# A chunk's input load in three column pieces of 48 rows instead of three row pieces of 16

## The chip, the cores and the metric

The kernel runs on one core of one Trainium2 chip. The core has five engines that run their own instruction lists: TensorE (PE, matrix products; its weight loads are listed as PEld), VectorE (DVE), ScalarE (ACT), GpSimd (POOL) and SyncE (SP), which here issues nearly all DMA transfers. Engines wait for each other and for transfers on semaphores. The metric is the device time of one execution in microseconds (us).

## What is computed

A recurrent attention over 768 steps for 4 batches of 8 heads, and after it a gated layer on its output. The reference, cut to what matters (`w_in`, `w_spatial`, `b_spatial` and `w_out` are the layer's weights):

```python
# r, k, v, w, a, b: (4, 8, 768, 40); state: (B, H, 40, 40), zero at first
for t in range(S):
    y[:, :, t] = einsum('bhd,bhde->bhe', rt, state)
    Sa = einsum('bhde,bhe->bhd', state, at)
    state = state * wt[:, :, None, :] - einsum('bhd,bhe->bhde', Sa, bt)
    state = state + einsum('bhd,bhe->bhde', vt, kt)
x = y.transpose(0, 2, 1, 3).reshape(B, S, H * D)
h = maximum(x @ w_in, 0)
u, v = h[..., :512], h[..., 512:]
v_n = (v - mean(v)) / sqrt(var(v) + 1e-6)          # over the last axis
v_s = einsum('ts,bsd->btd', w_spatial, v_n) + b_spatial[None, :, None]
out = (u * v_s) @ w_out
```

## The kernel before

The recurrence is done in chunks of 64 steps. There are two groups of two batches and 12 chunks each, so 24 chunks, `s` = 0 to 23; a chunk holds 8 units of a batch and a pair of heads, and the two heads of a pair (`par` 0 and 1) lie on the two halves of the partitions, from 0 and from 64 on, in 40 rows each.

Each chunk goes through three kinds of work. The **preparation** (`scan1`, `scan2`, `scr_store`, `at_mul`, `sl_mul`, `lprime`, `lblock`) takes the chunk's input tile `ein` (128 x 2064 floats): columns 0 to 527 (`W`) are the decays, the next 512 the vectors a, the last 1024 the vectors b and k. `scan1` (L288) and `scan2` (L297) run over the decays on VectorE, `at_mul` (L314) multiplies the a columns with the result, `sl_mul` (L320) the last columns, and `lprime` (L335) makes 32 x 32 blocks of their products on TensorE, which ScalarE copies out (`lblock`, L345). Every four chunks VectorE inverts these blocks in some 60 small steps (`invert`, L351 to L373). The **b_ work** makes the chunk's matrices, and the **c_ work** carries the state on from chunk to chunk: `c_bp` (L532), `c_ff` (L550), `c_xx` (L568), `c_mp` (L596, L607) and `c_y` (L618, L631), with copies on ScalarE and masks on GpSimd (`strict`, L405). Decoding of the weights and the first product of the gated layer (L676 to L739) are put in between, and a second phase (L100 to L202), on TensorE above all, follows.

There are four `ein` buffers for chunks 0 to 3. From chunk 4 on two are used in turn, `ein0` for even and `ein1` for odd chunks. Chunks 4 and 5 are loaded whole by `prep_load` (L270). From chunk 6 on `prep_piece` (L275) loads a chunk in six DMAs of SP: `k % 2` is the half of the partitions, `k // 2` the third of it. The pieces of chunk `q + 2` go into the buffer that chunk `q` leaves, so they are planned behind `sl_mul` of chunk `q`.

The order on each engine is set by the planned times in `at(t, ...)`: all calls are sorted by `t` and written out in that order. One unit of `t` is one chunk of the c_ work. The preparation of chunks 4 to 11 is planned two chunks per unit, later ones one per unit. SP works off its DMAs in order and stands still at one whose semaphores aren't there yet, for what its target is still read for and for an earlier DMA that used the same one of eight semaphores.

Of the kernel before, what the change touches and what calls it, by code (L numbers as in the profile page):

```python
# [19 lines left out]
C = 64  # L20
# [4 lines left out]
NU = NB * NP  # L25
GS = 4
WSEG = C + 2
WF = NU * WSEG
EW = WF + 3 * NU * C
# [187 lines left out]
def phase1(ctx, tc, early, late, vtok, win, xs, vns, uts, dscr):  # L217
    nc = tc.nc
# [32 lines left out]
    ein = [p.tile([P, EW], F32, name=f"ein{i}") for i, p in enumerate((pin, pin, extra, extra))]  # L251
# [18 lines left out]
            queues[par].dma_start(out=t[o:o + rows, cols], in_=early[par, s, 0:rows, cols])  # L270

    def prep_piece(s, k):
        par, r = k % 2, k // 2 * 16
        o = par * 64 + r
        nc.sync.dma_start(out=ein[s % 2][o:o + 16], in_=early[par, s, r:r + 16])  # L275

    def scan1(s, i=None):
        t = ein[s % 2 if i is None else i]
# [529 lines left out]
    for q in range(GS, NS):  # L808
        t = PREP.get(q, q - 8 + 0.01)
        at(OV.get((scan1, q), t + 0.20), scan1, q)  # L810
        at(OV.get((scan2, q), t + 0.28), scan2, q)
        at(OV.get((scr_store, q), t + 0.285), scr_store, q)
        at(OV.get((at_mul, q), t + 0.29), at_mul, q, AT_ENG)
        at(OV.get((sl_mul, q), t + 0.30), sl_mul, q, SL_ENG)
        if q + 2 < NS:
            gap = GAP.get(q, 0.07 if q < 12 else 0.14)
            for k in range(6):
                at(max(t + 0.40, OV.get((sl_mul, q), 0) + 0.01) + gap * k, prep_piece, q + 2, k)
        at(t + LPQ.get(q, LPO), lprime, q)
        at(t + LPQ.get(q, LPO) + 0.05, lblock, q)  # L820
# [168 lines left out]
```

## Time and profile before

| | |
|---|---|
| Time, median of 3 runs | 661.7 us (660.37, 661.7 and 666.66) |
| Profiled execution | 664.58 us, of which the span of the trace is 662.9 us |
| Busy share of the span | PE 87%, PEld 79%, DVE 67%, ACT 59%, POOL 34% |
| Mean granted TensorE clock | 0.941 of full speed |
| DMA | 87.68 MB in 106,587 packets, mean 132 GB/s |
| Chunk pieces (L275) | 108 DMAs of 129.0 KB |

How to read it: the busy shares are averages over the whole execution, whose stages have different limits, so a stage is looked at by itself. A matmul's end is modelled, so a busy TensorE isn't one at its peak. [...] An idle time in brackets stands just before the row's instruction, with what ended it.

### The profile page before, as it was taken

Reading aid. Unit: us, or ns where it says so; the run is one execution under the profiler, and the core shown is the slowest. Engines: PE = TensorE matmul, PEld = TensorE weight load, DVE = VectorE, ACT = ScalarE, POOL = GpSimd, SP = SyncE. Lnnn points to the kernel's source line nnn. Section 1 sums busy time; section 2 is a strip of 40 time slices with the busy share of each in tenths; the row PEclk is TensorE's granted clock in tenths of the full one; section 3 lists DMA queues with packets and bytes.
Section 4 is the critical chain, followed back from the end, with each engine's and each line's share of the span. In section 5 each row is a group of like instructions: output and inputs, shape, how many; then the busy total and the mean of one; then the engine's idle time right before and its main releaser. Section 6 shows DMA issues by size and latency. Waiting matters only on the chain.

```text
span 662.9 us, 25888 instructions
## 1 busy us (share of the span) xinstructions
PE 577.4 (87%) x10960; PEld 523.0 (79%) x10960; DVE 445.2 (67%) x951; ACT 394.3 (59%) x884; POOL 225.2 (34%) x312
## 2 busy tenths in 40 slices
PE   1628876478788888999999999999999999999998
PEld 1527766367677777888888888888888999999997
DVE  8898559978999999689787666443375844322221
ACT  2226654358676777788878888888774643232112
POOL 3113213104323334352341342323344935352121
PEclk9977787869798889999999999999999999999999
DMA  8754866458574756656666356365386558150001
GB/s 201 125 101 65 137 140 128 91 123 137 125 160 120 147 111 141 133 141 147 158 179 179 82 144 172 83 168 164 100 238 196 170 165 250 49 169 31 31 30 60
DMA packets 106587, 87.68 MB, mean 132 GB/s; under 512 B 35752, under 2 KB 92328, under 8 KB 104552
## 3 DMA queue, kind: packets, MB, share of 16 engines
q1 hardware_dynamic: 105928, 84.31, 52.4%
q10 hardware_dynamic: 544, 1.72, 1.1%
q8 instruction: 86, 1.41, 1.0%
q14 instruction: 29, 0.24, 0.1%
HBM read 59.20 MB, written 20.50 MB: 120 GB/s over the span
## 4 chain that ended last, share of the span: by engine, by line
PE 67%; DVE 13%; issue 7%; ACT 5%; DMA 5%; SPq 2%; POOL 1%; DVEq 0%; ACTq 0%; POOLq 0%
PE po L199 6%; PE pv L736 6%; PE pv L689 6%; PE pg L179 5%; PE pg L181 5%; PE pg L180 5%; PE bp L532 5%; PE ch L550 4%; PE ch L568 4%; PE bk L422 3%; PE bk L438 3%; DVE itmp L362 3%; PE bk L398 3%; DMA ein<-in_early 3%; DVE A L366 2%
## 5 line engine op out<-in xcount | busy, mean ns | idle before, releaser
L405 POOL TENSOR_SCALAR_AFFINE_SELECT Rt<-Rt 64x512 f32<-64x512 f32 (+1 forms) x144 | 83.8, 583 | 149.1 <-ACT Rt L578 113.6
L405 POOL TENSOR_SCALAR_AFFINE_SELECT At<-At 64x512 f32<-64x512 f32 x48 | 40.3, 840 | 149.9 <-ACT At L414 137.5
L362 DVE TENSOR_TENSOR itmp<-A 128x30 f32<-128x30 f32 (+9 forms) x180 | 68.7, 382 | 3.5
L542 ACT ACTIVATE Rt<-bp 64x416 f32<-64x416 f32 x96 | 49.1, 512 | 35.0 <-PE bp L532 33.2
L179 PE MATMUL pg<-wsh,vh 128*128 128x384 f32 x192 | 64.5, 336 | 1.1 <-ACT vh L51 1.1
L183 DVE TENSOR_TENSOR g<-pg,bb 128x384 f32<-128x384 f32 x32 | 17.8, 556 | 70.6 <-PE pg L181 67.9
L180 PE MATMUL pg<-wsl,vh 128*128 128x384 f32 x192 | 64.4, 335 | 0.0
L366 DVE TENSOR_TENSOR A<-A,itmp 128x30 f32<-128x30 f32 (+9 forms) x180 | 59.1, 328 | 6.1
L181 PE MATMUL pg<-wsh,vl 128*128 128x384 f32 x192 | 63.1, 336 | 0.0
L532 PE MATMUL bp<-lin,Mc 40*64 40x104 f32 x768 | 47.7, 280 | 16.7 <-DVE y L631 14.2
L532 PEld LDWEIGHTS bp<-lin,Mc 40*64 40x64 f32 x768 | 40.9, 151 | 20.2 <-DVE y L631 17.1
L55 POOL TENSOR_TENSOR gl<-g,gh 128x384 fp32r<-128x384 f32 x32 | 33.7, 1056 | 57.5 <-ACT gh L51 57.5
L578 ACT ACTIVATE Rt<-ch 64x416 f32<-64x416 f32 x96 | 49.2, 512 | 5.1 <-PE ch L568 2.7
L550 PE MATMUL ch<-Rt,At 128*64 128x104 f32 x768 | 46.9, 281 | 3.4 <-issue 2.6
L51 ACT ACTIVATE gh<-g 128x384 fp32r<-128x384 f32 x32 | 16.7, 522 | 54.5 <-DVE g L184 54.5
L550 PEld LDWEIGHTS ch<-Rt,At 128*64 128x64 f32 x768 | 41.3, 155 | 7.5 <-issue 4.2
L335 PE MATMUL bk<-at,sl 64*32 64x32 f32 x1536 | 22.4, 208 | 28.1 <-DVE sl L320 15.9
L335 PEld LDWEIGHTS bk<-at,sl 64*32 64x32 f32 x1536 | 18.7, 119 | 31.4 <-issue 13.2
L568 PE MATMUL ch<-ffs,xf 64*64 64x104 f32 x768 | 43.2, 267 | 0.0
L55 POOL TENSOR_TENSOR vl<-raw,vh 128x512 fp32r<-128x512 f32 x24 | 31.7, 1333 | 29.4 <-ACT vh L51 27.3
L607 DVE TENSOR_TENSOR Mc<-ch,scn 104x160 f32<-104x160 f32 x44 | 18.6, 439 | 32.8 <-PE ch L596 26.2
L568 PEld LDWEIGHTS ch<-ffs,xf 64*64 64x64 f32 x768 | 38.3, 144 | 1.1
(128 smaller groups left out, 1508.7 us busy)
## 6 DMA issues: line engine op xcount, KB each, us to landing
ein<-in_early SPq DMA_DIRECT2D x108, 129.0 KB
lin<-in_late SPq DMA_DIRECT2D x48, 160.0 KB
At<-at SPq DMA_DIRECT2D x48, 128.0 KB
uts<-ur SPq DMA_DIRECT2D x48, 128.0 KB
vns<-vr SPq DMA_DIRECT2D x24, 256.0 KB
raw<-vns SPq DMA_DIRECT2D x24, 256.0 KB
ut<-uts SPq DMA_DIRECT2D x24, 256.0 KB
Rt<-in_vtok SPq DMA_DIRECT2D x48, 80.0 KB
```

Of the source, the lines that this page charges most:

```text
L55: eng.tensor_tensor(out=lo, in0=x, in1=hi.bitcast(F32), op=ALU.subtract)
L179: nc.tensor.matmul(pg, lhsT=vh[:, dc], rhs=w_h, start=(i == 0), stop=False)
L180: nc.tensor.matmul(pg, lhsT=vh[:, dc], rhs=w_l, start=False, stop=False)
L181: nc.tensor.matmul(pg, lhsT=vl[:, dc], rhs=w_h, start=False, stop=(i == NT - 1))
L362: nc.vector.tensor_tensor(out=tp, in0=A[:, k + 1:, k:k + 1].broadcast_to([P, m, k]), in1=A[:, k:k + 1, 0:k].broadcast_to([P, m, k]), op=AL ...
L366: nc.vector.tensor_tensor(out=A[:, k + 1:, 0:k], in0=A[:, k + 1:, 0:k], in1=tp, op=ALU.add)
L405: nc.gpsimd.affine_select(out=t, in_=t, pattern=[[0, k], [1, C]], base=0, channel_multiplier=-1, compare_op=ALU.is_gt, fill=0.0,)
L532: nc.tensor.matmul(bp[PR[par], q, :], lhsT=Mc[RR[par], n, :], rhs=li[RR[par], n, C:], start=(q == 0), stop=False, skip_group_check=True,)
L542: nc.scalar.activation(Rt[par][PR[par], gp, :], st["bp", g][PR[par]], AF.Copy)
L550: nc.tensor.matmul(ff[PR[1 - par], q, :], lhsT=At[par][:, n, :], rhs=Rt[par][:, n, :], start=True, stop=True,)
L568: nc.tensor.matmul(xx[ev, q, :], lhsT=xf[ev, n, :], rhs=ffs[ev, q, :], start=True, stop=True,)
L578: done = nc.scalar.activation(Rt[par][PR[par], gp], xx[PR[1 - par]], AF.Copy, scale=-1.0)
```

## The change

The six pieces of a chunk's load are cut in another way. Before, a piece was 16 of the 48 rows of one half, in full width (16 x 2064 floats, 132 KB). After, it is all 48 rows of one half in one of three ranges of columns: 528 for the scans, 512 for the first product, 1024 for the last one (101, 98 and 197 KB). The two halves still alternate, and each piece has the planned time that it had.

```diff
     def prep_piece(s, k):
-        par, r = k % 2, k // 2 * 16
-        o = par * 64 + r
-        nc.sync.dma_start(out=ein[s % 2][o:o + 16], in_=early[par, s, r:r + 16])
+        par, cols = k % 2, (slice(0, WF), slice(WF, WF + NU * C), slice(WF + NU * C, EW))[k // 2]
+        o = par * 64
+        nc.sync.dma_start(out=ein[s % 2][o:o + 48, cols], in_=early[par, s, 0:48, cols])
```

On SP, at the place where chunk 6 (`ein_120`) is loaded, the rows of before (-) and of the change (+); in brackets are the semaphores a DMA waits for, where DMAHW ones belong to earlier DMAs and DVE is VectorE:

```order
-L275 DMA ein_120<-in_early 16x2064 [waits DMAHW2_49,DVE_49]
-L275 DMA ein_120<-in_early 16x2064 [waits DMAHW3_49]
-L275 DMA ein_120<-in_early 16x2064 [waits DMAHW4_49]
-L275 DMA ein_120<-in_early 16x2064 [waits DMAHW5_49]
-L275 DMA ein_120<-in_early 16x2064 [waits DMAHW6_49]
-L275 DMA ein_120<-in_early 16x2064 [waits DMAHW7_49]
+L275 DMA ein_120<-in_early 48x528 [waits DMAHW2_49,DVE_49]
+L275 DMA ein_120<-in_early 48x528 [waits DMAHW3_49]
+L275 DMA ein_120<-in_early 48x512 [waits DMAHW4_49,DVE_49]
+L275 DMA ein_120<-in_early 48x512 [waits DMAHW5_49]
+L275 DMA ein_120<-in_early 48x1024 [waits DMAHW6_49,DVE_49]
+L275 DMA ein_120<-in_early 48x1024 [waits DMAHW7_49]
```

The six stay where they were; the wait for VectorE stood on the first of them alone and now stands on the first of each pair.

On VectorE, at the preparation of the same chunk:

```order
-L288 SCALAR_TENSOR_TENSOR S<-ein_120,ends 128x528 [waits DMAHW5_49,DMAHW4_49,DMAHW6_49,DMAHW3_49,DMAHW7_49,DMAHW2_49,Activation_49]
+L288 SCALAR_TENSOR_TENSOR S<-ein_120,ends 128x528 [waits DMAHW3_49,DMAHW2_49,Activation_49]
 L292 RECIPROCAL ends<-S 128x8 [waits DVE_49]
 L297 SCALAR_TENSOR_TENSOR Et<-ein_120,ends 128x528 [waits DVE_49]
-L314 TENSOR_TENSOR at<-ein_120,Et 128x512 [waits DVE_49]
-L320 TENSOR_TENSOR sl<-ein_120,S 128x1024
+L314 TENSOR_TENSOR at<-ein_120,Et 128x512 [waits DMAHW5_49,DMAHW4_49,DVE_49]
+L320 TENSOR_TENSOR sl<-ein_120,S 128x1024 [waits DMAHW7_49,DMAHW6_49]
```

The first scan waited for six transfers and now waits for two; the two products each wait for two of their own. The order of VectorE, TensorE, ScalarE and GpSimd is the same in both kernels.

## Rows read from the trace of the kernel before

**Rows 1.** Windows: busy us (x instructions) of each engine, granted clock, DMA share, GB/s.
```profile
core 0: us, PE busy (x) PEld busy (x) DVE busy (x) ACT busy (x) POOL busy (x), PEclk, DMA share, GB/s
65.00:95.00 30.00, 23.06 (x661) 20.44 (x651) 15.85 (x20) 17.42 (x40) 6.71 (x11) 0.86 0.81 138
95.00:130.00 35.00, 23.41 (x624) 20.57 (x622) 32.86 (x77) 16.52 (x39) 9.46 (x18) 0.82 0.58 119
...
207.00:240.00 33.00, 27.53 (x696) 24.56 (x698) 31.65 (x59) 22.46 (x52) 8.00 (x16) 0.79 0.55 123
...
280.00:340.00 60.00, 60.00 (x1500) 52.89 (x1496) 49.73 (x123) 50.60 (x119) 21.52 (x34) 1.00 0.62 151
```

**Rows 2.** VectorE's timeline, 55 to 118 us: start, us, instruction [idle before, releaser].
```profile
55.25 1.26 DVE L297 TENSOR_TENSOR_SCAN Et<-ein,ends 128x528 f32<-128x528 f32 x1
...
64.67 0.42 DVE L631 TENSOR_TENSOR y<-bp,Et 104x256 f32<-104x256 f32 x1 [0.67 <-PE bp L618]
67.01 1.26 DVE L288 TENSOR_TENSOR_SCAN S<-ein,ends 128x528 f32<-128x528 f32 x1 [1.92 <-DMA ein<-in_early]
...
70.44 1.69 DVE L320 TENSOR_TENSOR sl<-ein,S 128x1024 f32<-128x1024 f32 x1
73.44 1.26 DVE L288 TENSOR_TENSOR_SCAN S<-ein,ends 128x528 f32<-128x528 f32 x1 [1.30 <-DMA ein<-in_early]
...
82.52 0.44 DVE L607 TENSOR_TENSOR Mc<-ch,scn 104x160 f32<-104x160 f32 x1 [4.43 <-ACT zt L483]
...
95.16 1.95 DVE L351 STREAM_TRANSPOSE A<-Lc 128x1024 f32<-128x1024 f32 x1 [5.23 <-ACT Lc L345]
...
117.73 1.25 DVE L288 TENSOR_TENSOR_SCAN S<-ein,ends 128x528 f32<-128x528 f32 x1
```

**Rows 3.** VectorE's waits, 60 to 345 us: total us, times, longest us.
```profile
DVE S L288 <- DMA ein<-in_early: 3.2, 2, 1.9
```

**Rows 4.** TensorE's waits, 60 to 345 us, those marked "issue".
```profile
PE bk L335 <- issue: 8.7, 6, 2.1
...
PE ch L550 <- issue: 2.6, 1, 2.6
PE bp L532 <- issue: 2.0, 1, 2.0
...
PE bk L398 <- issue: 1.6, 1, 1.6
```

**Rows 5.** Queue q8 (packets, MB, share of 16 engines), 64:69 and 83:87 us.
```profile
q8 instruction: 1, 0.02, 2.1%
...
q8 instruction: 1, 0.02, 1.9%
```

**Rows 6.** The same queue, 50 to 56 us.
```profile
q8 instruction: 1, 0.02, 1.0%
```

**Rows 7.** Windows by what the DMA engines carry: last two columns DMA share, GB/s.
```profile
0.00:16.00 16.00, 2.50 (x128) 2.06 (x128) 13.24 (x21) 4.34 (x10) 6.59 (x15) 1.00 0.88 201
29.00:43.00 14.00, 9.02 (x168) 8.47 (x164) 12.86 (x34) 6.95 (x15) 2.67 (x4) 0.98 0.95 163
63.00:73.00 10.00, 7.76 (x225) 6.96 (x223) 6.45 (x8) 5.54 (x12) 4.38 (x5) 0.84 1.02 138
```

**Rows 8.** SP's timeline: start, us in all, DMA issues.
```profile
24.73 1.41 SPq L270 DMA_DIRECT2D ein<-in_early  x2
...
58.40 2.64 SPq L275 DMA_DIRECT2D ein<-in_early  x6
...
63.84 4.41 SPq L275 DMA_DIRECT2D ein<-in_early  x6
...
69.56 1.17 SPq L391 DMA_DIRECT2D At<-at  x2
...
103.23 4.78 SPq L275 DMA_DIRECT2D ein<-in_early  x4
```

**Rows 9.** TensorE's timeline, the chain product behind the first such wait.
```profile
69.59 2.96 PE L550 MATMUL ch<-Rt,At 128*64 128x104 f32 x32
```

**Rows 10.** Window of that product; the granted clock is third from the end.
```profile
70.00:72.00 2.00, 2.00 (x28) 2.00 (x26) 2.00 (x2) 1.56 (x4) 1.53 (x2) 0.50 0.86 108
```

## The prediction

> **What bounds the kernel now.** I read the table of windows first, to see which engine is full in which stretch; then the timelines of the engines where none is; then the waits; and last the DMA. By the windows [rows 1], VectorE is the limit from 95 to 130 us (busy 32.86 of 35) and from 207 to 240 (31.65 of 33). From 280 us TensorE is busy all the time at the full granted clock: an input load can't be felt there, except that all of it moves earlier or later in one piece. From 65 to 95 us neither is full: TensorE 23.06 of 30, VectorE 15.85, ScalarE 17.42. This is where a chunk's load could matter, and what is won there moves everything behind it.
>
> VectorE's timeline of this stretch [rows 2] shows four chunks' scans and products done sooner than the others need them: it waits 1.92 us and 1.30 us ahead of the first scans (L288) of chunks 6 and 7 for their loads, then 4.43 us for ScalarE behind TensorE, and 5.23 us for the last blocks of chunk 7. The 3.2 us are the only time from 60 to 345 us that a VectorE instruction is held by a chunk's load [rows 3].
>
> TensorE's largest idle time that no engine explains is marked "issue", that is, waiting for nothing that the profile shows: from 60 to 345 us nine places of up to 2.6 us, 8.7 + 2.6 + 2.0 + 1.6 = 14.9 us [rows 4]. I looked at what the DMA queues carried there. In two of these places, 64 to 69 us and 83 to 87 us, one packet of the queue q8, kind "instruction", 0.02 MB, was on its way, with 2.1% of 16 engines over 5 us, or 1.68 us, and 1.9% over 4 us, or 1.22 us [rows 5]. In the quiet stretch from 50 to 56 us such a packet takes 1.0% of 16 x 6 us, 0.96 us [rows 6]. I read this as TensorE running out of instructions and waiting for a block that shares the DMA engines with data: an inference, since the trace does not say whose block it is. [...]
>
> **The change, part by part.** *What moves.* A chunk's load is 2 x 48 x 8,256 B = 0.793 MB in six DMAs, before and after. No instruction on PE, DVE, ACT or POOL moves, and on SP each piece stays where it stood.
>
> *How fast the six go* [rows 7]. From 63 to 73 us the traffic is mainly 16-row pieces: 138 GB/s at a DMA share of 1.02, so a chunk takes 0.793 / 0.138 = 5.7 us. The kernel's first loads go in 48 and 64 rows, divided by columns, on two queues: 201 GB/s at a share of 0.88, or 228 at a full one. From 29 to 43 us, 48 rows of full width go out from one queue among small transfers: 163 GB/s at 0.95, or 172. The new pieces, 48 rows from one queue, lie between: 3.5 to 4.6 us a chunk. I take 4.6, since the single queue is what they share with the third row. [...]
>
> *Who waits for which piece.* The first scan waited for all six pieces; now it waits for two (0.203 MB), the first product for two more, the last product for the last two. Chunk 6: SP stood until the last product of chunk 4 and issued from 58.40 on [rows 8]. Now the first two need only chunk 4's second scan, over at 55.25 + 1.26 = 56.51, 1.9 us sooner; the last two still need the last product. With all six issued by about 60 and the 4.6 us, the last lands by 65, the first two long before. VectorE comes to the scan at 64.67 + 0.42 = 65.09, so the 1.92 goes. Chunk 7: SP reaches it at 63.84 behind small stores that don't change. The first two pieces have from there to 73.44 - 1.30 - 1.92 = 70.22, 6.4 us, for a quarter of the chunk: the 1.30 goes too.
>
> *What that is worth.* Nothing by itself. VectorE is through chunk 7 3.2 us sooner, but its next instruction is released at 82.52, so the idle 4.43 becomes 7.65. TensorE is through its chain product (L550) at 69.59 + 2.96 = 72.55 [rows 9], and its next, chunk 6's blocks (L335), needs the last product of chunk 6, over at 70.44 + 1.69 = 72.13. There is 0.4 us of cover: without the earlier scan TensorE could gain no more than that ahead of this point. With it the cover is 2.3, and what TensorE gains is kept.
>
> *What TensorE gains.* Shorter waits for blocks. The two packets I priced are 0.72 and 0.26 us longer than the quiet one, 0.5 in the mean; over nine places 4.4 us. Half of that I put down to the chunk loads, the rest to the other transfers: 2.2 us. The bounds are 0 (a block still meets the same bytes) and 14.9 (all nine waits gone). I stay near the low end, since the block's own 0.96 us remains in every one of them.
>
> *What it costs.* SP issues as many pieces as before, with three times the rows each. The old ones took 2.64 / 6 = 0.44 us where nothing held them. The nearest rows for the new: copies of 64 x 512 at 1.17 / 2 = 0.59 us, loads of 48 x 2064 at 1.41 / 2 = 0.70 [rows 8]. I take 0.55, nearer to the first, as row count and width are: 0.11 x 6 = 0.7 us of SP per chunk, at most 0.26 x 6 = 1.6, and 0 where SP is waiting anyway. What covers it: chunk 10's last piece is the first of the four at 103.23 us, its scan comes at 117.73 [rows 2, 8], 14 us later, of which landing takes up to 5.2 (the last piece of chunk 7 went out by 63.84 + 4.41 = 68.25, its scan ran at 73.44). By then 30 pieces have made SP 3.3 us late, at most 7.8, under the 9 that are free. Without that cover each us would cost one, since VectorE is the limit there. The added waits on the two products are for pieces that land while the scans run: 0.
>
> *Sum.* The profiled run took 664.6 us (span 662.9 and 1.7 around it); 664.6 - 2.2 = 662.4. It lay 2.9 above the median of the three timed runs, 661.7, so against these the forecast is 659.5.
>
> **The rivals.** *No gain at all.* The load lands earlier only into VectorE's idle time, and the blocks take as long as before. For it: the bytes are the same, and some of the nine waits fall where no chunk load runs. Against it: a chunk now leaves the engines free 1.1 us sooner. Time: 661.7. [...]
>
> *The clock comes along (faster).* [...] If shorter gaps kept the level up, 65 to 95 us would give back up to 30 x (1 - 0.86) = 4.2 us, and 207 to 240 us up to 33 x (1 - 0.79) = 6.9, about half of it, VectorE being full there: 659.5 - 4.2 - 3.5 = 651.8. Against it: TensorE also waits for other engines there, and these gaps stay.
>
> *Blocks wait longer (slower).* A DMA engine gets three rows of a piece in place of one, 3 x 4,096 = 12,288 B for the last product in place of 8,256. Suppose that it serves a piece to its end before it turns to a block. At the old 138 / 16 = 8.6 GB/s per engine this holds the block for 1.43 us in place of 0.96: 0.47 more, in nine places 4.2 us, so 661.7 + 4.2 = 665.9. [...] The case decides at 138 x 12,288 / 8,256 = 205 GB/s: a rate above frees the engine sooner than before, a rate below later. My 172 lies below, the 228 above. Against it: the other four pieces bring 6,336 and 6,144 B per engine, less than before. [...]
>
> **How the numbers follow.** Small gain, 656 to 661: 0.53. No gain, 661 to 664: 0.20. The clock, around 652: 0.15. Longer blocks, 665 to 672: 0.12. The three timed runs spread over 660.4 to 666.7, and about 1%, 6.6 us, is what a measurement of this kernel can tell from no change. Below 655.1 lies most of the clock case and the deep end of the first, 0.17; above 668.3 over half of the longer blocks, 0.07; within it 0.76. The range holds the first two cases with that spread and reaches into both others: 651.5 to 667.
>
> **What would show it.** Right: no first scan waits for a chunk's load, VectorE idle over 7 us ahead of the instruction at 82 us, more than 170 GB/s where a chunk's load runs, L275 at 0.5 to 0.6 us, and TensorE's "issue" waits from 60 to 345 us down from 14.9 to about 12.7 us. It would be wrong if these waits stay or go altogether, if the granted clock from 65 to 95 us moves from 0.86 by more than 0.05, or if VectorE waits for loads from 95 to 130 us.

## The result and the profile after

The changed kernel takes 655.1 us (median of 4 runs, 650.7 to 656.9) where the kernel before takes 664.2 (4 runs, 660.4 to 667.6): a ratio of 0.989, with an interval of 0.985 to 0.993. Five more rounds beside 16 runs of before gave 654.4 us and 0.9886, 0.985 to 0.992. So the change makes the kernel 1.1% faster. The forecast had the sign, the place and the kind of wait, and a third of the size (659.5 against 661.7, or 0.3%).

The profiled execution took 656.94 us, with a span of 655.2. Its windows, to be read against [rows 1] and the last row against [rows 7] (busy us and count of PE, PEld, DVE, ACT, POOL, then granted clock, DMA share, GB/s):

```profile
65.00:95.00 30.00, 27.87 (x936) 24.48 (x931) 23.46 (x37) 24.34 (x58) 12.78 (x23) 1.00 0.60 154
95.00:130.00 35.00, 20.41 (x506) 18.15 (x501) 33.30 (x68) 12.19 (x29) 4.51 (x9) 0.65 0.44 119
...
207.00:240.00 33.00, 26.88 (x790) 23.70 (x788) 31.62 (x65) 24.69 (x58) 12.18 (x21) 0.91 0.49 133
...
280.00:340.00 60.00, 60.00 (x1412) 52.29 (x1408) 51.01 (x122) 48.57 (x111) 23.07 (x35) 1.00 0.60 168
63.00:73.00 10.00, 9.19 (x321) 8.13 (x316) 9.23 (x12) 7.03 (x18) 5.75 (x5) 1.00 0.56 135
```

From 65 to 95 us TensorE now does 936 products where it did 661, at a granted clock of 1.00 where it was 0.86. (The clock records of both traces have 1.00 and 0.50 alone, so a value between them is a mean over the window.) In 63 to 73 us the DMA engines move 135 GB/s, about what they did, at a share of 0.56 in place of 1.02.

TensorE's waits from 54 to 345 us, the rows that answer to [rows 4] and the one DMA wait among them (total us, times, longest):

```profile
PE bk L335 <- issue: 2.5, 2, 1.5
PE ch L550 <- DMA Rt<-in_vtok: 1.6, 1, 1.6
```

The "issue" waits fell from 16.9 us at twelve places to 2.5 us at two. The 16.9 are the 14.9 of [rows 4] and two groups of the kernel before that are not shown there:

```profile
PE bp L618 <- issue: 1.8, 2, 1.3
PE bk L501 <- issue: 0.2, 1, 0.2
```

A new wait of 1.6 us appears: TensorE comes to the chain product L550 at 84 us sooner than a small load that it needs.

VectorE's timeline, to be read against [rows 2]:

```profile
65.69 1.36 DVE L288 TENSOR_TENSOR_SCAN S<-ein,ends 128x528 f32<-128x528 f32 x1
...
70.36 1.70 DVE L288 TENSOR_TENSOR_SCAN S<-ein,ends 128x528 f32<-128x528 f32 x1
...
77.20 0.44 DVE L607 TENSOR_TENSOR Mc<-ch,scn 104x160 f32<-104x160 f32 x1 [1.72 <-ACT Rt L578]
...
87.20 1.98 DVE L351 STREAM_TRANSPOSE A<-Lc 128x1024 f32<-128x1024 f32 x1 [2.58 <-ACT Lc L345]
```

The scans of chunks 6 and 7 wait for no load. The start of the second inversion (L351) is a good milestone, since VectorE is the limit from there on: 95.16 us before, 87.20 after, 8.0 us sooner, although the first inversion ended 0.7 us later here (50.79 against 50.12 us at its first result). The same instruction of the fourth inversion shows what is kept:

```profile
212.66 1.93 DVE L351 STREAM_TRANSPOSE A<-Lc 128x1024 f32<-128x1024 f32 x1
```

```profile
204.78 1.92 DVE L351 STREAM_TRANSPOSE A<-Lc 128x1024 f32<-128x1024 f32 x1
```

(before, then after): 7.9 us sooner. At the fifth it is 10.3 (282.03 to 271.75): between the two, "issue" waits of 5.8 us at four places have become 1.1 us at one. At the end of the span 7.7 are left; what took back 2.6 us from there on was not followed up. So 8.0 us, as much as is left at the end, are won from 54 to 95 us, the stretch that the forecast named.

### The profile page after: what moved, and what is told of

The parts are those of the page before. It is cut to its first block, busy times and chain, and to the rows that moved or that the text cites. A ratio compares the mean times of both kernels' runs of the same rounds, so it can differ in the third digit from the quotient of the medians.

```text
span 655.2 us, 25918 instructions
## 1 busy us (share of the span) xinstructions
PE 574.2 (88%) x10960; PEld 520.7 (79%) x10960; DVE 441.6 (67%) x951; ACT 392.9 (60%) x884; POOL 225.1 (34%) x312
## 3 DMA queue, kind: packets, MB, share of 16 engines
q10 hardware_dynamic: 544, 1.72, 1.2%
## 4 chain that ended last, share of the span: by engine, by line
PE 66%; DVE 13%; issue 6%; DMA 6%; ACT 5%; SPq 3%; POOL 1%; ACTq 0%; DVEq 0%; POOLq 0%
PE po L199 6%; PE pv L736 6%; PE pv L689 6%; PE pg L179 5%; PE pg L180 5%; PE pg L181 5%; PE ch L550 4%; PE ch L568 4%; PE bp L532 4%; DMA ein<-in_early 3%; PE bk L422 3%; PE bk L438 3%; DVE itmp L362 2%; PE bk L398 2%; PE bp L618 2%
## 5 line engine op out<-in xcount | busy, mean ns | idle before, releaser
L405 POOL TENSOR_SCALAR_AFFINE_SELECT Rt<-Rt 64x512 f32<-64x512 f32 (+1 forms) x144 | 82.3, 572 | 142.9 <-ACT Rt L578 110.6
L405 POOL TENSOR_SCALAR_AFFINE_SELECT At<-At 64x512 f32<-64x512 f32 x48 | 42.3, 881 | 146.8 <-ACT At L414 126.0
L362 DVE TENSOR_TENSOR itmp<-A 128x30 f32<-128x30 f32 (+9 forms) x180 | 67.2, 373 | 3.5
L532 PE MATMUL bp<-lin,Mc 40*64 40x104 f32 x768 | 47.6, 279 | 21.4 <-DVE y L631 20.9
L532 PEld LDWEIGHTS bp<-lin,Mc 40*64 40x64 f32 x768 | 40.7, 151 | 25.1 <-DVE y L631 24.3
L550 PE MATMUL ch<-Rt,At 128*64 128x104 f32 x768 | 47.9, 284 | 1.8 <-DMA Rt<-in_vtok 1.6
L550 PEld LDWEIGHTS ch<-Rt,At 128*64 128x64 f32 x768 | 42.3, 157 | 5.9 <-issue 3.2
L568 PE MATMUL ch<-ffs,xf 64*64 64x104 f32 x768 | 42.3, 263 | 0.0
L335 PE MATMUL bk<-at,sl 64*32 64x32 f32 x1536 | 21.2, 206 | 22.5 <-DVE sl L320 19.9
L607 DVE TENSOR_TENSOR Mc<-ch,scn 104x160 f32<-104x160 f32 x44 | 18.6, 439 | 31.5 <-PE ch L596 23.7
L179 PEld LDWEIGHTS pg<-wsh,vh 128*128 128x128 f32 x192 | 36.6, 191 | 2.3 <-ACT vh L51 2.1
L335 PEld LDWEIGHTS bk<-at,sl 64*32 64x32 f32 x1536 | 18.0, 117 | 25.4 <-DVE sl L320 13.0
```

The costliest lines, as they stand in the source:

```text
L179: nc.tensor.matmul(pg, lhsT=vh[:, dc], rhs=w_h, start=(i == 0), stop=False)
L362: nc.vector.tensor_tensor(out=tp, in0=A[:, k + 1:, k:k + 1].broadcast_to([P, m, k]), in1=A[:, k:k + 1, 0:k].broadcast_to([P, m, k]), op=AL ...
L405: nc.gpsimd.affine_select(out=t, in_=t, pattern=[[0, k], [1, C]], base=0, channel_multiplier=-1, compare_op=ALU.is_gt, fill=0.0,)
L532: nc.tensor.matmul(bp[PR[par], q, :], lhsT=Mc[RR[par], n, :], rhs=li[RR[par], n, C:], start=(q == 0), stop=False, skip_group_check=True,)
L550: nc.tensor.matmul(ff[PR[1 - par], q, :], lhsT=At[par][:, n, :], rhs=Rt[par][:, n, :], start=True, stop=True,)
L568: nc.tensor.matmul(xx[ev, q, :], lhsT=xf[ev, n, :], rhs=ffs[ev, q, :], start=True, stop=True,)
```

## The experiments

Which of three properties of the new pieces does it: that the first scan waits for fewer of them, that their rows are short, or that their rows lie on other partitions at the same moment? And is it really blocks of instructions that TensorE waits for? To price the loads I use the share of 16 DMA engines that queue q1 takes, times the span, less that of a kernel without the chunk loads (experiment 4), over 18 chunks. This is an estimate: it takes the other traffic's time as unchanged. The rows of before and after, from the page's list of queues (packets, MB, share):

```profile
q1 hardware_dynamic: 105928, 84.31, 52.4%
```

```profile
q1 hardware_dynamic: 109384, 84.31, 47.5%
```

These are 347.4 and 311.2 us of all 16 engines.

### 1. Spread rows in full width

```diff
-        par, r = k % 2, k // 2 * 16
-        o = par * 64 + r
-        nc.sync.dma_start(out=ein[s % 2][o:o + 16], in_=early[par, s, r:r + 16])
+        par, r = k % 2, k // 2
+        o = par * 64
+        nc.sync.dma_start(out=ein[s % 2][o + r:o + 48:3], in_=early[par, s, r:48:3])
```

> Kernel before, but a piece takes every third of the 48 rows of a half (rows r, r+3, ...) instead of 16 adjacent ones; still 16 rows of 8,256 B in full width, same count, order and waits. If it is the spread over the partitions that makes the load fast: time about 655 (ratio 0.99), DMA share from 63 to 73 us near 0.6, TensorE's issue waits from 60 to 345 us near 2.5 us. If it is the length of the rows: as before, 664, share 1.0, issue waits about 15 us. If it is that the first scan waits for fewer pieces: as before too, with 3 us of waits of the first scans.

Measured: 655.4 us, ratio 0.989 (0.984 to 0.994). Issue waits 4.1 us, 47.3% of 653.5 us for q1, the second inversion at 88.03 us. VectorE still waits 2.1 us for all six pieces of a chunk:

```profile
DVE S L288 <- DMA ein<-in_early: 2.1, 2, 1.3
```

So the whole gain comes with rows as long as before, as many of them, and most of the first scans' old waits (3.2 us); only which 16 rows go together is changed. Neither short rows nor fewer pieces to wait for are needed.

### 2. 48 adjacent rows in full width

```diff
+        if k > 1:
+            return
+        o = k * 64
+        nc.sync.dma_start(out=ein[s % 2][o:o + 48], in_=early[k, s, 0:48])
```

> Kernel before, but a chunk's load is two DMAs of 48 rows in full width (8,256 B a row), at the times of the first two pieces. If long rows are slow: share and issue waits as before, 660 to 665 (four issues less per chunk). If few adjacent rows are slow: as after, 655. If the scans' waits matter: as before, 664, since the first scan waits for all and SP stands until the last product.

Measured: 677.8 us, ratio 1.021 (1.015 to 1.027). Issue waits 32.6 us at fourteen places, up to 4.2:

```profile
PE bk L336 <- issue: 12.3, 5, 3.1
PE bp L619 <- issue: 8.4, 2, 4.2
```

A chunk costs (51.4% of 678.9 - 259.4) / 18 = 5.0 us of all engines, as much as in 16-row pieces. 48 rows alone do not help: long rows of adjacent partitions stay slow, and with two DMAs a chunk TensorE's waits are twice those with six (16.9). Why they double was not tested, and the slowdown was no theory's expectation.

### 3. The three column ranges in reverse

```diff
-        ...(slice(0, WF), slice(WF, WF + NU * C), slice(WF + NU * C, EW))[k // 2]
+        ...(slice(0, WF), slice(WF, WF + NU * C), slice(WF + NU * C, EW))[2 - k // 2]
```

> Kernel after, with the three column ranges in reverse: the last product's columns are loaded first, the decays last, so SP stands until the last product as before, and the first scan waits for the last pieces. Transport theory (rows or spread): nearly as after, 655 to 657, with issue waits near 2.5 us. Theory of the earlier scans: back to 662 to 664, the first scans of chunks 6 and 7 waiting 1 to 3 us.

Measured: 656.4 us, ratio 0.990 (0.984 to 0.995). No first scan waits for a load. TensorE's issue waits are 7.2 us, more than the 2.5 expected. With SP held until the last product, and the decays loaded last, nearly all of the gain is there. The earlier scans are worth at most what lies between 0.990 and 0.989, which these intervals do not tell from nothing.

### 4. No chunk loads

```diff
     def prep_piece(s, k):
+        return
```

> Kernel before without the loads of chunks 6 to 23 (their preparation works on the data of chunks 4 and 5): the price of all chunk loads from 60 us on. If the change took away nearly all that the loads cost: 653 to 655, as after, and the same few issue waits. If half of it is still there: 648 or less.

Measured: 651.5 us, ratio 0.983 (0.978 to 0.987). q1 falls to 70.04 MB and 39.9% of 650.2 us, 259.4 us:

```profile
q1 hardware_dynamic: 102472, 70.04, 39.9%
```

So all chunk loads together cost the kernel before some 1.7%, and 1.1% of it is what the change takes away. The 14.3 MB cost (347.4 - 259.4) / 18 = 4.9 us a chunk before, and (311.2 - 259.4) / 18 = 2.9 us after. The time lies between the two that were expected. Issue waits of 2.2 us remain without any chunk load, about as many as after the change.

### 5. 16 adjacent rows in halves of the columns

```diff
+        for cols in (slice(0, EW // 2), slice(EW // 2, EW)):
+            nc.sync.dma_start(out=ein[s % 2][o:o + 16, cols], in_=early[par, s, r:r + 16, cols])
```

> Kernel before, but each piece of 16 adjacent rows goes as two DMAs of half the columns (4,128 B a row): short rows, few partitions, twelve issues per chunk, first scan waits for all. If long rows are slow: DMA share from 63 to 73 us 0.6 to 0.7, issue waits 2 to 5 us, time 655 to 659. If few adjacent partitions are slow: share 1.0 and issue waits about 15 us as before, 664 or more.

Measured: 669.8 us, ratio 1.013 (1.008 to 1.018). Shorter rows go faster on the same 16 adjacent partitions: 48.2% of 667.2 us gives 3.5 us a chunk, between 4.9 and 2.9, and the issue waits fall to 5.6 us. (The run changes the number and size of the DMAs along with the rows, so the row length isn't shown by itself.) But the time is longer than before, as other transfers come late; that SP's twelve issues per chunk make them late is the likely reason, not a tested one:

```profile
DVE S L289 <- DMA Rt<-in_vtok: 6.9, 1, 6.9
DVE S L289 <- DMA ein<-in_early: 4.8, 2, 4.2
DVE S L289 <- DMA scr<-sc: 2.4, 1, 2.4
```

VectorE's first scans now wait 14.1 us in all, where it was 3.2. So the time is lost in waits for data, not in TensorE's issue waits.

### 6 and 7. Traffic that nobody waits for

Behind each piece of chunks 6 to 18 of the kernel after, a DMA into a tile that nothing reads, in one run as before had it, in the other in the new form:

```diff
+        r = k // 2 * 16
+        if s <= 18:
+            nc.sync.dma_start(out=st["spare"][o + r:o + r + 16], in_=early[par, s, r:r + 16])
```

```diff
+        if s <= 18:
+            nc.sync.dma_start(out=st["spare"][o:o + 48, cols], in_=early[par, s, 0:48, cols])
```

> Kernel after, plus, behind each piece of chunks 6 to 18, a piece of 16 adjacent rows of 8,256 B as before had it, into a tile that nothing reads. Blocks theory: TensorE's issue waits come back (10 to 20 us from 60 to 245 us), the granted clock of 65 to 95 us falls below 0.9, 662 to 670, although no instruction waits for these transfers. If TensorE's waits had another cause: 655 to 658 and no such waits.

> The same extra bytes and as many extra DMAs as in the run before this one, but as 48 rows in the three column ranges. Theory of long rows or few partitions: much less harm, 656 to 660, issue waits 3 to 8 us. If extra bytes or extra issues of SP are what counts: as much as the other, 662 to 670.

Measured: 683.2 us and 1.034 (1.029 to 1.039) for the old form; 668.6 us and 1.009 (1.006 to 1.013) for the new one. Issue waits from 60 to 345 us are 14.9 and 10.8 us, where the kernel after has 2.5. So transfers on which no instruction depends bring these waits back, and the same bytes in as many DMAs do 2.4% less harm in the new form. Both times lie above what was expected for their theories, and the second (668.6) in the range named for extra bytes or issues, so extra traffic costs in either form. The runs are no clean price of the blocks: with SP's issues doubled, TensorE also waits for a small load behind them, 19.1 us at four places and 10.9 at two, and VectorE waits for loads 23.8 and 13.6 us in all from 60 to 345 us, where the kernel after has no such wait.

```profile
PE ch L553 <- DMA Rt<-in_vtok: 19.1, 4, 8.2
```

```profile
PE ch L553 <- DMA Rt<-in_vtok: 10.9, 2, 7.1
```

### 8. The changed kernel again

> The changed kernel once more in five rounds, for its ratio: 0.985 to 0.993 by every theory.

Measured: 654.4 us, 0.9886 (0.985 to 0.992); issue waits of 6.4 us in this execution, and the second inversion at 86.62 us. So the same kernel has 2.5 us of these waits in one execution and 6.4 in another, with the milestone at nearly the same time.

### 9 and 10. Reading spread, writing spread

Experiment 1 changes which rows of memory are read and which partitions are written. Apart:

```diff
+        par, r = k % 2, k // 2
+        o = par * 64 + r * 16
+        nc.sync.dma_start(out=ein[s % 2][o:o + 16], in_=early[par, s, r:48:3])
```

```diff
+        par, r = k % 2, k // 2
+        o = par * 64
+        nc.sync.dma_start(out=ein[s % 2][o + r:o + 48:3], in_=early[par, s, r * 16:r * 16 + 16])
```

> Kernel before, but a piece reads every third of the 48 rows in memory (r, r+3, ...) and still writes 16 adjacent partitions; the rows of chunks 6 to 23 land in another order than the computation wants, so its values are changed. If what made the interleaved pieces fast is the partitions that are written: as before, ratio 0.995 to 1.005, issue waits of TensorE from 60 to 345 us 12 to 20 us. If it is the rows that are read: 0.99, issue waits 2 to 5 us.

> The other half: 16 adjacent rows of memory are read, and every third partition is written (values changed as in the run before this one). If the written partitions matter: ratio 0.99, issue waits 2 to 5 us. If the rows that are read matter: as before, 0.995 to 1.005 and 12 to 20 us.

Measured: reading spread 662.0 us, ratio 0.999 (0.995 to 1.003), 4.4 us a chunk; writing spread 654.5 us, ratio 0.988 (0.983 to 0.993), 2.9 us a chunk. Issue waits 9.5 and 3.4 us; the 9.5 lie below the 12 to 20 that were expected with the time as before. The list of DMA packets in the traces shows the same without any subtraction. Each row of 8,256 B is a packet of its own, 1,728 for 18 chunks of 96 rows. It took 692 ns in the mean in the kernel before, 650 with only the reads spread, 480 with only the writes spread, 482 with both (experiment 1) and 719 as 48 adjacent rows (experiment 2). The gain is on the side of the partitions that are written. The number of rows in a DMA does not decide by itself, since experiment 2 writes 48 adjacent rows and stays slow (5.0 us a chunk).

### 11. Are they blocks of instructions?

32 small products more on TensorE, where it stands idle ahead of 52 us:

```diff
+        def pe_fill(n):
+            pv = ps_m.tile([P, DH], F32, name="pv")
+            for _ in range(n):
+                nc.tensor.transpose(pv[:, 0:P], ident, ident)
+        at(0.415, pe_fill, 32)
         at(0.42, b_zt, 0)
```

> Kernel before with 32 more small products on TensorE (transposes of the identity into a tile that nobody reads), in the stretch from 38 to 52 us where TensorE stands idle. If the issue waits are waits for instruction blocks of a fixed length, each comes 32 products earlier in the work: the one before L398 of chunk 2 moves to the start of L532 or the end of L335 ahead of it, the one 62 products into L335 of chunk 6 to about 30 into it, the one 12 into L335 of chunk 8 to about 12 into L618 before it, the one 11 into L550 to about 11 into L398 before it. If these waits belong to what the instructions need (data, buffers), they stay where they are. Time 658 to 668 in both cases.

Measured: 663.7 us, ratio 1.001 (0.997 to 1.005). TensorE's timeline around the four waits, first of before:

```profile
68.51 1.15 PE L398 MATMUL bk<-at,sl 64*64 64x64 f32 x32 [1.62 <-issue]
...
74.45 0.22 PE L335 MATMUL bk<-at,sl 64*32 64x32 f32 x2 [1.02 <-issue]
...
86.35 0.65 PE L335 MATMUL bk<-at,sl 64*32 64x32 f32 x52 [1.21 <-issue]
...
92.45 1.20 PE L550 MATMUL ch<-Rt,At 128*64 128x104 f32 x21 [2.57 <-issue]
```

and with the 32 products:

```profile
68.22 1.38 PE L532 MATMUL bp<-lin,Mc 40*64 40x104 f32 x26 [2.37 <-issue]
...
82.28 0.58 PE L618 MATMUL bp<-Rt,tk 128*40 128x64 f32 x13
83.83 0.76 PE L618 MATMUL bp<-Rt,tk 128*40 128x64 f32 x19 [0.97 <-issue]
...
88.48 0.80 PE L398 MATMUL bk<-at,sl 64*64 64x64 f32 x20 [1.58 <-issue]
```

The first moved from the start of L398 to the start of L532, 32 products ahead. The third moved from 12 products into L335 to 13 into L618, the fourth from 11 into L550 to 12 into L398 (20 of 32 still to come). The second is not there at all. A wait for data would have stayed with its data: these belong to a count of instructions. Counting by the timeline of before, 126 products lie from the first to the second, 254 to the third, 127 to the fourth, and each is a weight load and a product. With TensorE's semaphore instructions, which the trace lists too, the count is exact: in all 14 traces every issue wait from 54 to 345 us, 120 in all, ends at instruction 256 n + 192 or 193 of TensorE's list.

The blocks are also those of queue q8, which the prediction could only infer. TensorE's list in the kernel before has 22,090 instructions and q8 86 packets, 257 to a packet; experiment 12 has 176 more, and 87 packets. And each of the 120 waits ends 1.2 to 2.1 us after the n-th packet of q8 has landed. The packets run one block ahead: from 60 to 285 us none starts more than 0.9 us before TensorE enters the block ahead of its own.

### 12. TensorE kept busy in its idle stretch

Experiment 11's edit on the kernel after, with 88 products.

> Kernel after with 88 such products in the same idle stretch, so that TensorE is busy until its next real product at 53 us. If the granted clock follows, the products from 53 to 62 us (L568 3.04 us) run in about half the time and the stretch to 65 us ends 1 to 3 us earlier: ratio to before 0.983 to 0.988. If VectorE or GpSimd set the end there: as after, 0.9886.

Measured: 662.9 us, ratio 0.999 (0.996 to 1.003): the gain of the change is gone. The products ended too soon:

```profile
36.53 9.77 PE L923 MATMUL pv<-ident 128*128 128x128 f32 x88
53.22 1.06 PE L474 MATMUL bk<-XT,l 32*32 32x32 f32 x32 [6.92 <-DVE XT L371]
...
85.30 0.32 PE L335 MATMUL bk<-at,sl 64*32 64x32 f32 x12 [2.00 <-issue]
```

TensorE stood idle for 6.92 us again, and its granted clock was 0.50 from 54 to 65 us, where the kernel after has 0.68. A block wait of 2.00 us came at 83.3, where the block that began 11 products into L550 now begins, 88 products earlier. This run changes both, the clock and the places of the blocks, but experiment 1 had 0.50 in the same stretch and kept the gain. Product L618 and the second inversion, first of experiment 1, then of this run:

```profile
80.57 1.09 PE L618 MATMUL bp<-Rt,tk 128*40 128x64 f32 x32
88.03 1.95 DVE L351 STREAM_TRANSPOSE A<-Lc 128x1024 f32<-128x1024 f32 x1
```

```profile
81.61 1.09 PE L618 MATMUL bp<-Rt,tk 128*40 128x64 f32 x32
92.29 1.97 DVE L351 STREAM_TRANSPOSE A<-Lc 128x1024 f32<-128x1024 f32 x1 [4.55 <-ACT Lc L345]
```

At L618 this run is 1.0 us later, as it was from 52 us on; at the inversion 4.3. The 3.3 us between come with the block wait of 2.00 us and slower products behind it (the next L550 takes 2.25 us, in experiment 11 1.65), not with the low clock before. Of the 7.6 us at the end of the span, what came behind this point was not followed up. It was no test of the clock, and no version that beats the changed kernel.

## Why the prediction was right, and where its size came from

**The time: in the range, partly by luck.** A ratio of 0.989 on the 661.7 us that the forecast started from is 654.5 us, below the 656 to 661 of the favoured case and near the 652 of the clock case. The range held it because it reached into that rival. Of the prediction's own signs of being right, one held: no first scan waits for a load. One held in part: the transfers went at 222 GB/s from 60 to 63 us, over 170, but at 135 from 63 to 73. The others failed: VectorE was idle 1.72 us ahead of its product (L607) and not over 7, as TensorE's part came 5.3 us sooner; L275 took 0.446 us and not 0.5 to 0.6; the issue waits went to 2.5 us and not to 12.7. And a sign of being wrong came true: the clock from 65 to 95 us moved by 0.14, more than 0.05.

**What bounds the kernel: right.** The stretch from 54 to 95 us is where the gain was made, and 7.7 to 8 us of it are still there at the end.

**How fast the six go: right in kind, too small.** Forecast 5.7 to 4.6 us a chunk; by q1's share, another measure, 4.9 to 2.9 us (experiment 4). I took 172 GB/s, the row of 48 full-width rows from one queue, for the nearest. Experiment 2 shows that this row was the slow kind itself: such a load costs 5.0 us a chunk. The two-queue row (3.5 us) was the nearer one.

**Who waits for which piece: right, and rightly priced at nothing.** The first scans' 3.2 us are gone. Experiment 1 keeps 2.1 us of them and the gain too; experiment 3 loads the decays last, and loses next to nothing.

**What TensorE gains: the step that failed in size.** 2.2 us were forecast of 14.9, which left three of the twelve places out; of 16.9 us, 10.5 (experiment 8) to 14.4 went. The failing sentences are those that price a wait by the packet's own time: half of the packets' excess, and "the block's own 0.96 us remains in every one of them". The packets run one block ahead (experiment 11), and most blocks bring no wait: from 54 to 345 us of the kernel before 50 came, and twelve waits arose. At the four waits from 66 to 93 us the same four blocks compare like this, from the traces' lists of packets and instructions (us):

| Wait before, and its end | Packet starts after TensorE has entered the block ahead: before, after | Packet takes: before, after |
|---|---|---|
| 1.62, at 68.51 | 2.67, 0.15 | 1.67, 1.31 |
| 1.02, at 74.45 | 2.88, 0.35 | 1.60, 1.09 |
| 1.21, at 86.35 | 2.29, 0.88 | 1.20, 1.23 |
| 2.57, at 92.45 | 2.89, 1.84 | 1.68, 1.50 |

So the packets take 0.26 us less in the mean, but they start 1.9 us sooner, and none of the four waits is left. That start is the term that the prediction's sum didn't have. Over 60 to 285 us it is 1.3 us in the mean before and 0.9 after, by the measure of the table; the packets take 1.28 and 1.12, in experiment 2 1.29, and without the chunk loads 1.09. What holds a packet's start no view shows. The packets of the first and the third row after the change, to be read against [rows 5], are these:

```profile
q8 instruction: 1, 0.02, 2.0%
```

```profile
q8 instruction: 1, 0.02, 1.9%
```

(63 to 67, and 76 to 80 us, so 1.28 and 1.22 us against 1.68 and 1.22.)

**The clock: a rival that paid in one of its two places.** Its condition was that shorter gaps keep the level up. From 65 to 95 us it rose from 0.86 to 1.00, and from 207 to 240 from 0.79 to 0.91. The second gave nothing back: VectorE was full there, and the fourth inversion starts 7.9 us sooner and its first result comes 7.5 us sooner (270.70 to 263.17). From 95 to 130 us, where VectorE is full too, the level fell from 0.82 to 0.65. The chain product of [rows 9], which ran at 0.50 before [rows 10], shows what the first gave:

```profile
68.14 1.86 PE L550 MATMUL ch<-Rt,At 128*64 128x104 f32 x32
```

1.86 us in place of 2.96; the next one, L568, 1.64 in place of 2.94 at 77.26 us. I had held against it that TensorE waits for other engines there; ahead of L568 that wait, 0.53 us, is the same in both kernels (up to 75.78 before, 71.81 after), but after the change the low clock did not follow it: 1.00 from 71 to 76 us, where it was 0.59 from 76 to 79 before. The 8.0 us at the second inversion are made up, as far as the timelines show, of the four block waits (6.4), less the new 1.6, and of 2.4 from these two products; the rest is some 1.5 when the 0.7 later start is counted. Of it 1.0 lies in two L335 and one L455 of the same passage (1.17, 1.08 and 0.96 us before, 0.76, 0.76 and 0.69 after).

**What it costs: less than taken.** L275 took 446 ns at the median in place of 439, not 550. Three times the rows do not show on SP.

**Blocks wait longer: did not happen.** The rate needed, 205 GB/s at a full share, is passed: 135 GB/s at 0.56 would be 241 at a full one, an estimate. Three rows a DMA engine in place of one was an even split of 48 rows and of 16 over 16 engines; one each fits the trace of before, where at most 17 packets of 8,256 B are in flight at once. Whether an engine serves a piece to its end before a block was the prediction's supposition, and no run shows it: in both kernels each row of a piece is a packet of its own (after the change 1,728 of 2,112 B for the decays of 18 chunks of 96 rows). The top of this case, 672, lies 6 us above the 665.9 that the longer blocks give, for products at the low clock behind longer waits. No run shows that term: with 32.6 us of issue waits, experiment 2 has a granted clock of 0.91 from 65 to 95 us, where the kernel before has 0.86.

**No gain at all: did not happen**, though it would have been right had the loads' own arrival been the point.

**The sum.** 662.4 was forecast for a profiled run against 664.6; it was 656.9. The waits' size and the clock with them are the difference, and the chance of 0.17 for more than 1% was too low for what the clock's row showed.

## What to carry to other kernels

Look at what the DMA engines do to transfers that no instruction names: here, at a DMA share near 1 (1.02 from 63 to 73 us) and with small products on TensorE, waits for blocks of instructions took 16.9 us from 54 to 345 us, and the trace shows each as a wait for nothing, at a multiple of 256 instructions from the others, give or take one. Where a load of long rows is cut into pieces, try pieces whose rows are written to partitions apart from each other; here a stride of three on the same pieces did as much as the new division by columns (0.989 and 0.989). And price a fetch that runs ahead by whether it brings a wait, as twelve of 50 did here, not by how long it takes.

## What was not expected of the hardware

- The written side decides: spread reads 0.999, spread writes 0.988. A chunk of 0.793 MB costs all 16 engines, by q1's share, 4.9 us in 16 adjacent rows of 8,256 B (4.4 with the reads spread), 2.8 to 2.9 us with every third partition written, 3.5 us in 16 adjacent rows of 4,128 B, 2.9 us in the new pieces, 3.2 us in the new pieces in reverse, and 5.0 us as 48 adjacent rows of 8,256 B. Why 48 adjacent long rows are as slow as 16, and 48 adjacent short ones are not, no run here shows.
- A block's packet can land over a microsecond before TensorE goes on: 1.2 to 2.1 us, at all 120 waits. In the kernel before the one ahead of 74.45 us had landed at 73.00, 0.43 us before its wait of 1.02 us began.
- 88 small products in an idle stretch took back a gain of 1.1%, without lying on any path themselves; of the 4.3 us up to the second inversion, 3.3 came with a block wait of 2.00 us, at a block that began 88 products earlier in the work, and the slower products behind it.
